# The last pair's second product: another order of the seven block products, one subtraction in two halves, one store issued from ScalarE

## The chip, the cores and the metric

The kernel runs on one core of one Trainium2 chip. The metric is the device time of one execution in microseconds (us), smaller is better. The kernel before has a median of 206.29 us over 6 runs (205.96 to 207.04).

## What is computed

Two stages follow each other. Attention with 4 batches, 8 heads, 768 tokens and head width 64: each token sees the 96 tokens up to itself and the first 8 tokens of its sequence, with a penalty that grows with distance. Then a feed-forward block on the 3072 tokens of width 512:

```
h = x @ w_in              # 3072 x 512  @  512 x 2048
g = h - np.tanh(h)
out = g @ w_out           # 3072 x 2048 @ 2048 x 512
```

The change touches the last line only, and of it the last 256 of the 3072 tokens.

## The kernel before, in words

The tokens are cut into 24 tiles of 128. The first four tiles go through the feed-forward block alone, the other twenty in ten pairs. A pair makes `g` (2048 x 256, bf16) in eight steps: TensorE (PE) multiplies by `w_in`, ScalarE (ACT) takes tanh, VectorE (DVE) subtracts.

The second product of a pair is done as two-by-two blocks with seven products in place of eight (function `by_strassen`). Let G(t,r) be tile t's part of `g` for half r of the 2048 rows, W(r,c) the block of `w_out` for row half r and column half c (256 of 512 columns). DVE first makes five sums of G blocks (operations ("A", g, kk), function `a_sum`, tile `hb`); the sums of W blocks (`bsum`) were made once, early. Then PE makes the products, 8 matmuls each into a PSUM bank:

- P4 = G(1,1)(W(1,0) - W(0,0)) and P3 = G(0,0)(W(0,1) - W(1,1)), in one bank, "in"
- P1 = (G(0,0) + G(1,1))(W(0,0) + W(1,1)), bank "one"
- P5 = (G(0,0) + G(0,1))W(1,1) and P2 = (G(1,0) + G(1,1))W(0,0), in one bank, "mid"
- P7 = (G(0,1) - G(1,1))(W(1,0) + W(1,1)); P6 = (G(1,0) - G(0,0))(W(0,0) + W(0,1)). In the last pair P7 has a bank of its own ("out2"), and P6 is made in two halves of 128 columns each, in two banks ("out" and "out3").

The blocks of the output are put together by a chain of operations, all but the first on DVE, each with a name in the code (key of the planner's operation):

- "s34" (ACT): copy P3 and P4 to `sum`. "t": tsum = P3 + P4. "u": tsum = P1 + tsum.
- "cx": the two cross blocks of the output, P5 + P3 and P2 + P4, 512 columns, into `ot2`.
- "ab": `sum` = tsum - cross, 512 columns: what is still missing in the two other blocks is only P7 and P6.
- "cs": the two other blocks, `ot2` = P7 or P6 + `sum`. In the last pair there are three: "out2" (256 columns, P7), "out" and "out3" (128 columns each, the halves of P6).
- Stores: in the last pair one of the two cross blocks after "cx" (256 KB, line 565), and one after each "cs" (128 KB, 64 KB, 64 KB, line 568). All are issued from SyncE's queue (SP). In the profile all DVE operations of this chain have line 324 and all matmuls of the products line 354, since helpers record them.

The order on each engine is not written by hand. A planner (class `Planner`) takes every operation with its engine, an assumed duration, what it comes after and which buffers it takes, and lays out a timetable; the instructions are then emitted engine by engine in that order. Order among the seven products is fixed by a list, ORDER = (4, 3, 1, 5, 2, 7, 6).

Of the kernel before, what the change touches and what calls it, by code (L numbers as in the profile page):

```python
# [13 lines left out]
PE, ACT, DVE, POOL, SP = ENG.PE, ENG.Activation, ENG.DVE, ENG.Pool, ENG.SP  # L14
# [158 lines left out]
def kernel(  # L173
# [11 lines left out]
    nc = tc.nc  # L185

    B, H, S, Dh = q.shape
    P = 128
# [41 lines left out]
    pl = Planner()  # L230
# [55 lines left out]
    DH = DM // 2  # L286
    LAST = len(groups) - 1
# [35 lines left out]
    def add(e, out, x, sign, y):  # L323
        eng_of(e).tensor_tensor(out=out, in0=x, in1=y, op=ALU.add if sign > 0 else ALU.subtract)  # L324
# [231 lines left out]
        assert r1 > r0  # L556
        nc.sync.dma_start(out=dst, in_=buf("ot2", ("ot2", g)))

    def store_part(g, part, c0=0, c1=DH):
        r0, r1 = [(tiles[u][0] * NQ + tiles[u][1]) * P for u in pair(g)]  # L560
        row = out.ap[0][0]
        src = buf("ot2", ("ot2", g))
        if part == "cross":
            dst = bass.AP(out.tensor, out.offset + r0 * row + DH, [[row, P], [(r1 - r0) * row - DH, 2], [1, DH]])
            nc.sync.dma_start(out=dst, in_=src.rearrange("q a d -> q (a d)")[:, DH : 3 * DH].rearrange("q (a d) -> q a d", a=2))
        else:
            r = (r0, r1)[part]
            nc.sync.dma_start(
                out=out[r : r + P, part * DH + c0 : part * DH + c1], in_=src[:, part, part * DH + c0 : part * DH + c1],
            )  # L570

# [19 lines left out]
    for g, us in enumerate(groups):  # L591
# [7 lines left out]
        out=ident, in0=rel, scalar1=0.0, scalar2=None, op0=ALU.is_equal), after=[("rel",)], pri=-3)  # L599
# [3 lines left out]
    for m in range(3):  # L603
        for half in range(2):
            pl.op(("mk", m, half), ACT, 0.85 if m or half else 2.15, lambda e, m=m, half=half: build_mask(m, half),
                  after=[("dist", m), ("mk", 0, 1) if m == 1 else None],
                  pri=-2 if m == 0 else 1)
# [4 lines left out]
    for it in arrive:  # L612
        nm, j = it[0], int(it[1:])
        if nm == "i":
            key = ("in", j)
            c0, w = in_from[j] * P, IN_PARTS[j]
            pl.op(key, POOL, 0.8, lambda e, j=j, c0=c0, w=w: nc.gpsimd.dma_start(  # L617
                out=w_in_bf[j], in_=w_in_r[:, :, c0 : c0 + w * P]),
                  after=[prev and ("issue", prev)], dma=T_W * w / 4 + (0.5 if j == 0 else 0.0) + (0.1 if w < 4 else 0.0), lag=W_LATE)
            prev = key  # L620
        elif nm == "o":
            key = ("out", j)
            pl.op(key, POOL, 0.8, lambda e, j=j: nc.gpsimd.dma_start(out=w_out_bf[j], in_=w_out_r[:, j * FJ : (j + 1) * FJ, :]),  # L623
                  after=[prev and ("issue", prev)], dma=T_W, lag=W_LATE)
            prev = key
        else:
            u = j
            src = {"k": k, "q": q, "v": v}[nm]
            key = ("ld", nm, u)
# [6 lines left out]
            if (nm, u) in hw_loads:  # L636
# [4 lines left out]
                          out=dst8(buf("kf", ("kf", nm, u)).rearrange("p h d -> p (h d)")) if u < N8 else buf("kf", ("kf", nm, u)),  # L641
# [4 lines left out]
                      lambda e, u=u, nm=nm, dst=dst: copy(e, dst(), buf("kf", ("kf", nm, u))),  # L646
# [12 lines left out]
    for u in range(NU):  # L659
# [64 lines left out]
        g = group_of[u]  # L724
# [16 lines left out]
                      out=buf(xname(g), ("xT", g))[:, :, off : off + P], in_=buf("x", ("x", u)).rearrange("q h d -> q (h d)")),  # L741
                  after=[("N", u, 0), ("N", u, 1), ("issue", prevx) if prevx else None], take=xt, give=[("x", u)], dma=T_TR, lag=LATE, pri=-1)

    ORDER = (4, 3, 1, 5, 2, 7, 6)
    for kk in (6, 4, 3, 1, 7):
        for j in range(2):
            pl.op(("B", kk, j), [(DVE, 0.602)], None, lambda e, kk=kk, j=j: b_sum(e, kk, j),
# [12 lines left out]
    def by_strassen(g):  # L760
        us = pair(g)
        per = shape1(g)[1] if g < PAIR0 else BANK // P
        p2 = 2 if g < PAIR0 else 1.5
        u0, u1 = us
        heads = [g] if g < PAIR0 else us
        gall = [("g", x, f) for x in heads for f in range(0, CF, per)]
        glow = [("g", x, f) for x in heads for f in range(0, CH, per)]
        for tag in gtags(g):
            pl.uses[tag] = 7
        for kk in (6, 1, 5, 2, 7):  # L770
            pl.op(("A", g, kk), [(DVE, 0.602)], None, lambda e, g=g, kk=kk: a_sum(e, g, kk),
                  after=glow if kk == 6 else gall, take=[("hb", ("a", g, kk))], give=gtags(g), pri=1)
        before_p = {4: gall, 3: [], 1: [("A", g, 1)], 5: [("A", g, 5)], 2: [("A", g, 2)],
                    7: [("A", g, 7)], 6: [("A", g, 6)]}
        last = None
        for kk in ORDER:
            bs = [("B", kk, j) for j in range(2)] if kk in B_OF else []
            n = home(g, kk)[0]
            opens = kk in (4, 1, 5, 7) or g == LAST and kk == 6
            halves = [0, 1] if g == LAST and kk == 6 else [1]  # L780
            for half in halves:
                two = len(halves) == 2
                key = ("P", g, kk) if half else ("Pp", g, kk)
                tag = "out3" if two and half else n
                c = (half * DH // 2, half * DH // 2 + DH // 2) if two else (0, DH)
                pl.op(key, PE, 0.45 if two else 0.875, lambda e, g=g, kk=kk, c=c, tag=tag: product(g, kk, c[0], c[1], tag),
                      after=before_p[kk] + bs + ([("issue", last)] if last else []),
                      take=[("bank", ("P", g, tag))] + ([("lim2", ("l2", g, n))] if g != LAST or kk in (4, 1, 5) else []) if opens else [],
                      give=(gtags(g) if kk in A_RAW else [("a", g, kk)]) if half else [], pri=p2, mode="full")
                last = key  # L790

        def bank(g, n):
            return buf("bank", ("P", g, n)).rearrange("q (a d) -> q a d", a=2)

        def one(g):
            return buf("bank", ("P", g, "one"))[:, 0:DH]

        def cross(g):
            return buf("ot2", ("ot2", g)).rearrange("q a d -> q (a d)")[:, DH : 3 * DH].rearrange("q (a d) -> q a d", a=2)

        def same(g):
            return bass_same(buf("ot2", ("ot2", g)))

        def sm(g):
            return buf("sum", ("s", g))

        def ts(g):
            return buf("tsum", ("t", g))

        pl.op(("s34", g), [(ACT, 0.483), (DVE, 0.6)], None, lambda e, g=g: copy(e, sm(g), bank(g, "in")),  # L810
              after=[("P", g, 3), ("P", g, 4)], take=[("sum", ("s", g))], give=[("P", g, "in"), ("l2", g, "in")], pri=1)
        pl.op(("t", g), DVE, 0.335, lambda e, g=g: add(e, ts(g), sm(g)[:, 0, :], 1, sm(g)[:, 1, :]),
              after=[("s34", g)], take=[("tsum", ("t", g))], pri=1)
        pl.op(("u", g), DVE, 0.335, lambda e, g=g: add(e, ts(g), one(g), 1, ts(g)),
              after=[("t", g), ("P", g, 1)], give=[("P", g, "one"), ("l2", g, "one")], pri=1)
        pl.op(("cx", g), DVE, 0.605, lambda e, g=g: add(e, cross(g), bank(g, "mid"), 1, sm(g)),
              after=[("P", g, 5), ("P", g, 2), ("s34", g)], take=[("ot2", ("ot2", g))],
              give=[("P", g, "mid"), ("l2", g, "mid")], pri=1)
        pl.op(("ab", g), DVE, 0.6, lambda e, g=g: add(
            e, sm(g), ts(g).rearrange("q (a d) -> q a d", a=1).to_broadcast([P, 2, DH]), -1, cross(g)),  # L820
              after=[("cx", g), ("u", g)], give=[("t", g)], pri=1)
        if g == LAST:
            pl.op(("st", u0), SP, 0.6, lambda e, g=g: store_part(g, "cross"), after=[("cx", g)], dma=T_ST)
            for t, c0, c1, key, tag in ((0, 0, DH, ("P", g, 7), "out2"), (1, 0, DH // 2, ("Pp", g, 6), "out"),
                                        (1, DH // 2, DH, ("P", g, 6), "out3")):
                end = tag == "out3"
                pl.op(("cs", g, tag), DVE, 0.335 if t == 0 else 0.2, lambda e, g=g, t=t, c0=c0, c1=c1, tag=tag: add(
                    e, buf("ot2", ("ot2", g))[:, t, t * DH + c0 : t * DH + c1], buf("bank", ("P", g, tag))[:, c0:c1], 1, sm(g)[:, t, c0:c1]),
                      after=[("ab", g), key], give=[("P", g, tag)] + ([("s", g)] if end else []), pri=1)
                pl.op(("st", us[t], tag), SP, 0.4, lambda e, g=g, t=t, c0=c0, c1=c1: store_part(g, t, c0, c1), after=[("cs", g, tag)],  # L830
                      give=[("ot2", g)] if end else [], dma=T_ST * (c1 - c0) / DM)
            return
        pl.op(("cs", g), DVE, 0.605, lambda e, g=g: add(e, same(g), bank(g, "out"), 1, sm(g)),
              after=[("ab", g), ("P", g, 7), ("P", g, 6)], give=[("P", g, "out"), ("l2", g, "out"), ("s", g)], pri=1)
        pl.op(("st", u0), SP, 0.6, lambda e, g=g: store2(g), after=[("cs", g)], give=[("ot2", g)], dma=2 * T_ST)
# [52 lines left out]
    seq2, share2 = [], []  # L888
    for g, us in enumerate(groups):
        if fast(g):  # L890
            seq2 += [("P", g, kk) for kk in ORDER]
            share2 += [us[0] + 2.0 * n / 7 for n in range(7)]
        elif g >= HEAD:
            for t in range(len(us)):
                n = 5 if us[t] == NU - 1 else 4
                seq2 += [("m2", g, t, qq) for qq in range(n)]
                share2 += [us[t] + qq / n for qq in range(n)]
# [61 lines left out]
```

## Time and profile before

| | us |
|---|---|
| median of 6 runs | 206.29 |
| the profiled execution's own time | 206.01 |
| its span, first to last instruction | 204.2 |
| PE busy over the span | 197.5 |
| DVE busy over the span | 183.8 |
| from 196.0 to 200.0: PE, DVE, ACT busy | 4.00, 3.24, 0.59 |
| from 200.0 to 204.2: PE, DVE, ACT busy | 0.35, 0.86, 0.00 |

The profile counts time from the span's start; the execution's own time is 1.8 us longer than its span. The columns of a timeline are start, duration, engine, line and operation, and out<-in by the program's names. A name with a q behind the engine (SPq) is the engine's queue that issues a DMA: the duration there is that of issuing, not of the transfer. Merged lines (x3) hold several instructions, from the first one's start to the last one's end. In the last stretch of the span, from 200.0 to 204.2, almost no engine computes.

### The profile page before, as it was taken

Reading aid. Unit: us, or ns where it says so; the run is one execution under the profiler, and the core shown is the slowest. Engines: PE = TensorE matmul, PEld = TensorE weight load, DVE = VectorE, ACT = ScalarE, POOL = GpSimd, SP = SyncE. Lnnn points to the kernel's source line nnn. Section 1 sums busy time; section 2 is a strip of 40 time slices with the busy share of each in tenths; the row PEclk is TensorE's granted clock in tenths of the full one; section 3 lists DMA queues with packets and bytes.
Section 4 is the critical chain, followed back from the end, with each engine's and each line's share of the span. In section 5 each row is a group of like instructions: output and inputs, shape, how many; then the busy total and the mean of one; then the engine's idle time right before and its main releaser. Section 6 shows DMA issues by size and latency. Waiting matters only on the chain.

```text
span 204.2 us, 6062 instructions
## 1 busy us (share of the span) xinstructions
PE 197.5 (97%) x2397; PEld 169.7 (83%) x2400; DVE 183.8 (90%) x408; ACT 138.8 (68%) x326; POOL 67.1 (33%) x83
## 2 busy tenths in 40 slices
PE   7999999999999999999999999999999999999992
PEld 5669989478798989888889888889888889888882
DVE  6799989999799899999898999898999899799683
ACT  5888889266796678559986548986648967534310
POOL 8993665360455310725040735040630000000000
PEclk9999999999999999999999999999999999999999
DMA  6999999999799995999998999996999222102023
GB/s 139 165 195 190 171 199 203 180 157 174 206 129 184 106 105 153 110 136 228 103 109 151 112 164 187 113 108 152 109 161 170 55 51 106 27 6 99 2 106 103
DMA packets 104429, 27.18 MB, mean 133 GB/s; under 512 B 94800, under 2 KB 101584, under 8 KB 104400
## 3 DMA queue, kind: packets, MB, share of 16 engines
q0 software_dynamic: 72416, 13.37, 86.5%
q1 hardware_dynamic: 31184, 13.11, 32.6%
q10 hardware_dynamic: 800, 0.30, 0.7%
q8 instruction: 19, 0.31, 0.6%
q14 instruction: 10, 0.08, 0.2%
HBM read 27.30 MB, written 6.29 MB: 164 GB/s over the span
## 4 chain that ended last, share of the span: by engine, by line
PE 79%; DMA 12%; POOL 5%; DVE 1%; issue 1%; DVEq 0%; POOLq 0%
PE bank L497 34%; PE bank L354 33%; DMA w_out_bf<-in_moe_w_out_dram 7%; DMA w_in_bf<-in_moe_w_in_dram 5%; PE bank L425 5%; PE bank L445 2%; PE bank L538 2%; PE bank L447 2%; POOL vb L654 2%; POOL w_in_bf L617 1%; POOL kb L652 1%; POOL qb L652 1%; DVE ot L324 1%; PE bank L482 0%; POOL w_out_bf L623 0%
## 5 line engine op out<-in xcount | busy, mean ns | idle before, releaser
L497 PE MATMUL bank<-xT,w_in_bf 128*128 128x256 bf16 (+1 forms) x896 | 93.3, 257 | 0.0
L497 PEld LDWEIGHTS <-w_in_bf 128*128 128x128 bf16 x896 | 76.1, 98 | 7.7
L850 ACT ACTIVATE th<-bank 128x512 f32<-128x512 f32 x96 | 57.3, 610 | 35.0 <-PE bank L497 33.2
L506 DVE TENSOR_TENSOR g<-bank,th 128x512 bf16<-128x512 f32 x80 | 53.4, 684 | 7.5 <-ACT th L850 6.4
L354 PEld LDWEIGHTS <-hb 128*128 128x128 bf16 x464 | 43.7, 98 | 5.6
L654 POOL DMA_DIRECT2D kb<-in_k_dram x20 | 17.7, 887 | 75.4 <-PE bank L497 59.0
L354 PE MATMUL bank<-bsum,hb 128*128 128x256 bf16 (+1 forms) x288 | 35.5, 270 | 0.0
L324 DVE TENSOR_TENSOR hb<-g 128x1024 bf16<-128x1024 bf16 x50 | 32.6, 686 | 0.4
L430 ACT ACTIVATE pd<-bank 128x512 bf16<-128x512 f32 x48 | 26.1, 599 | 7.5 <-PE bank L425 7.4
L354 PE MATMUL bank<-w_out_bf,hb 128*128 128x256 bf16 x176 | 22.7, 273 | 0.0
L654 POOL DMA_DIRECT2D vb<-in_v_dram x24 | 21.4, 895 | 2.3 <-DMA w_out_bf<-in_moe_w_out_dram 2.2
L430 ACT ACTIVATE po<-bank 128x512 bf16<-128x512 f32 x40 | 22.0, 614 | 0.0
L462 ACT ACTIVATE x<-bank,rden 128x64 bf16<-128x64 f32 x88 | 20.4, 326 | 2.0 <-DVE rden L454 1.7
L354 PE MATMUL bank<-bsum,g 128*128 128x256 bf16 x160 | 20.2, 273 | 0.0
L435 DVE TENSOR_TENSOR pd<-pd,mk 128x1024 bf16<-128x1024 bf16 (+1 forms) x30 | 17.0, 578 | 1.9 <-ACT pd L430 1.6
L654 POOL DMA_DIRECT2D qb<-in_q_dram x20 | 17.7, 888 | 0.9 <-PE bank L482 0.8
L354 PEld LDWEIGHTS <-g 128*128 128x128 bf16 x160 | 15.1, 98 | 2.4
L324 DVE TENSOR_TENSOR ot<-bank,sum 128x512 f32<-128x512 f32 (+2 forms) x24 | 15.2, 638 | 0.8 <-PE bank L354 0.6
L445 PE MATMUL bank<-vb,pd 128*128 128x65 bf16 x192 | 14.6, 193 | 0.6 <-DVE pd L435 0.5
L425 PE MATMUL bank<-qT,kT 64*128 64x128 bf16 x352 | 13.8, 217 | 0.6 <-DVE qT L415 0.6
L425 PEld LDWEIGHTS <-kT 64*128 64x128 bf16 x352 | 10.0, 94 | 4.9 <-issue 4.1
L435 DVE TENSOR_TENSOR po<-po,mk 128x1024 bf16<-128x1024 bf16 (+1 forms) x23 | 14.0, 616 | 0.0
(66 smaller groups left out, 178.2 us busy)
## 6 DMA issues: line engine op xcount, KB each, us to landing
out_dram<-ot SPq DMA_DIRECT2D x10, 512.0 KB, 4.4
vb<-in_v_dram POOLq DMA_DIRECT2D x24, 128.0 KB, 5.9
kb<-in_k_dram POOLq DMA_DIRECT2D x23, 128.0 KB, 4.7
qb<-in_q_dram POOLq DMA_DIRECT2D x23, 128.0 KB, 5.3
w_in_bf<-in_moe_w_in_dram POOLq DMA_DIRECT2D x4, 512.0 KB, 9.5
w_out_bf<-in_moe_w_out_dram POOLq DMA_DIRECT2D x4, 512.0 KB, 12.8
out_dram<-ot SPq DMA_DIRECT2D x3, 256.0 KB, 2.3
xT<-x SPq DMA_TRANSPOSE x18, 2.5
```

What stands on the lines that cost most here:

```text
L324: eng_of(e).tensor_tensor(out=out, in0=x, in1=y, op=ALU.add if sign > 0 else ALU.subtract)
L354: nc.tensor.matmul(o, a, b[:, c0:c1], start=(f == 0), stop=(f == CH - 1))
L425: nc.tensor.matmul(t[hh][:, p * P : (p + 1) * P], kt[r, p, :], qt[r, p, :], start=True, stop=True)
L430: nc.scalar.activation(dst, t, AF.Exp, bias=0.0, scale=scale)
L435: nc.vector.tensor_tensor(out=p, in0=p, in1=mk[:, m, s0 * NP : s1 * NP, :], op=ALU.mult)
L445: nc.tensor.matmul(o, pd[:, slot(h), :], vd[:, h, 0 : Dh + 1], start=True, stop=w is None)
L447: nc.tensor.matmul(o, buf("po", ("p", u, 1))[:, slot(h), :], bufs[vname(w)][got["vb", w]][:, h, 0 : Dh + 1], start=False, stop=True,)
L462: nc.scalar.activation(x[:, h, :], t[:, h, 0:Dh], AF.Copy, bias=0.0, scale=rd[:, h, :])
L497: nc.tensor.matmul(t[:, (f - fa) * n : (f - fa + 1) * n], w_in_bf[j][:, c, fo : fo + P], xt[:, c, 0:n], start=(c == 0), stop=(c == CD - 1),)
L506: nc.vector.tensor_tensor(out=dst, in0=t.rearrange("q (b n) -> q b n", n=n), in1=th.rearrange("q (b n) -> q b n", n=n), op=ALU.subtract,)
L654: else nc.gpsimd.dma_start(out=dst(), in_=rows(src, u)),
L850: pl.op(("th", g, f), ACT, 0.48, lambda e, g=g, f=f: nc.scalar.activation(buf("th", ("th", g, f)), buf("bank", ("h", g, f)), AF.Tanh, bias ...
```

## The change

Three edits, all in the last pair:

1. The order of its products becomes 4, 3, 5, 2, 1, 7, 6: P1 comes after P5 and P2 in place of before them. The order of the DVE sums that feed them follows (6, 5, 2, 1, 7). The other pairs keep theirs.
2. "ab" becomes two operations of 256 columns each, one per tile; each "cs" waits for its own half only.
3. The store of "out" (the first half of P6) is issued from ACT's queue; the two other stores of line 568 stay with SP.

Counts: DVE has one instruction more, SP one DMA less, ACT one DMA more; PE has the same instructions, 24 of them in another order. On DVE the order of the chain is t, cx, u, ab (twice), cs (three times); before it is t, u, cx, ab, cs (three times). All instructions ahead of this chain keep their order.

```diff
-    def store_part(g, part, c0=0, c1=DH):
+    def store_part(g, part, c0=0, c1=DH, e=SP):
...
-            nc.sync.dma_start(
+            (nc.scalar if e is ACT else nc.sync).dma_start(
                 out=out[r : r + P, part * DH + c0 : part * DH + c1], in_=src[:, part, part * DH + c0 : part * DH + c1],
             )
...
-    ORDER = (4, 3, 1, 5, 2, 7, 6)
+    def order_of(g):
+        return (4, 3, 5, 2, 1, 7, 6) if g == LAST else (4, 3, 1, 5, 2, 7, 6)
+
...
-        for kk in (6, 1, 5, 2, 7):
+        for kk in (6, 5, 2, 1, 7) if g == LAST else (6, 1, 5, 2, 7):
...
-        for kk in ORDER:
+        for kk in order_of(g):
...
-        pl.op(("ab", g), DVE, 0.6, lambda e, g=g: add(
-            e, sm(g), ts(g).rearrange("q (a d) -> q a d", a=1).to_broadcast([P, 2, DH]), -1, cross(g)),
-              after=[("cx", g), ("u", g)], give=[("t", g)], pri=1)
         if g == LAST:
+            pl.uses["t", g] = 2
+            for t in range(2):
+                pl.op(("ab", g, t), DVE, 0.335, lambda e, g=g, t=t: add(e, sm(g)[:, t, :], ts(g), -1, cross(g)[:, t, :]),
+                      after=[("cx", g), ("u", g)], give=[("t", g)], pri=t)
...
-                      after=[("ab", g), key], give=[("P", g, tag)] + ([("s", g)] if end else []), pri=1)
-                pl.op(("st", us[t], tag), SP, 0.4, lambda e, g=g, t=t, c0=c0, c1=c1: store_part(g, t, c0, c1), after=[("cs", g, tag)],
+                      after=[("ab", g, t), key], give=[("P", g, tag)] + ([("s", g)] if end else []), pri=0.5)
+                pl.op(("st", us[t], tag), ACT if tag == "out" else SP, 0.4, lambda e, g=g, t=t, c0=c0, c1=c1: store_part(g, t, c0, c1, e), after=[("cs", g, tag)],
                       give=[("ot2", g)] if end else [], dma=T_ST * (c1 - c0) / DM)
             return
+        pl.op(("ab", g), DVE, 0.6, lambda e, g=g: add(
+            e, sm(g), ts(g).rearrange("q (a d) -> q a d", a=1).to_broadcast([P, 2, DH]), -1, cross(g)),
+              after=[("cx", g), ("u", g)], give=[("t", g)], pri=1)
```

More of the change, by code (lines that the diff above doesn't have):

```diff
@@ L890 @@
         if fast(g):
-            seq2 += [("P", g, kk) for kk in ORDER]
+            seq2 += [("P", g, kk) for kk in order_of(g)]
             share2 += [us[0] + 2.0 * n / 7 for n in range(7)]
```

## The prediction

> **What bounds the kernel now.** First the page's busy shares and its chain that ended last: PE is busy nearly throughout and carries 79% of that chain, so the body of the kernel is PE's. The change leaves every instruction ahead of the last pair's closing chain in place, so only the end can pay or cost. I therefore read the end of the chain in order of time:
>
> ```profile
> PE 197.5 (97%) x2397; PEld 169.7 (83%) x2400; DVE 183.8 (90%) x408; ACT 138.8 (68%) x326; POOL 67.1 (33%) x83
> PE 79%; DMA 12%; POOL 5%; DVE 1%; issue 1%; DVEq 0%; POOLq 0%
> ...
> 192.47 6.13 PE bank L354 x56
> 198.62 0.70 DVE ot L324
> 199.34 0.70 DVE sum L324
> 200.09 0.04 issue
> 200.14 0.42 DVE ot L324
> ```
>
> PE makes 56 matmuls, seven products of 6.13/7 = 0.876 us each, without a gap. At 198.62, as soon as P2 has ended, the chain leaves PE for DVE: "cx", "ab", "cs". Three products are still to come, and yet PE is no longer what ends last. The timeline of the same stretch shows by how little, and what follows:
>
> ```profile
> 196.00 0.59 ACT L413 COPY sum<-bank 128x512 f32<-128x512 f32 x1 [2.90 <-PE bank L354]
> 196.67 1.91 PE L354 MATMUL bank<-w_out_bf,hb 128*128 128x256 bf16 x16
> 197.05 0.42 DVE L324 TENSOR_TENSOR tsum<-sum 128x256 f32<-128x256 f32 x1
> 197.58 0.42 DVE L324 TENSOR_TENSOR tsum<-bank,tsum 128x256 f32<-128x256 f32 x1
> 198.42 1.93 PE L354 MATMUL bank<-bsum,hb 128*128 128x256 bf16 x24
> 198.62 0.69 DVE L324 TENSOR_TENSOR ot<-bank,sum 128x512 f32<-128x512 f32 x1 [0.62 <-PE bank L354]
> 199.34 0.69 DVE L324 TENSOR_TENSOR sum<-tsum,ot 128x512 f32<-128x512 f32 x1
> 200.14 0.42 DVE L324 TENSOR_TENSOR ot<-bank,sum 128x256 f32<-128x256 f32 x1
> 200.48 0.48 DVE L324 TENSOR_TENSOR ot<-bank,sum 128x128 f32<-128x128 f32 x2
> ```
>
> SP's own lines of that time, and from the view of DMA issues the time from issue to landing (the cross store, "out2", the two 64 KB stores):
>
> ```profile
> 200.59 0.34 SPq L568 DMA_DIRECT2D out_dram<-ot  x1
> 201.03 0.38 SPq L568 DMA_DIRECT2D out_dram<-ot  x1
> 201.50 0.41 SPq L568 DMA_DIRECT2D out_dram<-ot  x1
> ...
> out_dram<-ot SPq DMA_DIRECT2D x1, 256.0 KB, 2.2
> out_dram<-ot SPq DMA_DIRECT2D x1, 128.0 KB, 1.7
> out_dram<-ot SPq DMA_DIRECT2D x2, 64.0 KB, 1.6
> ```
>
> Three things to see. PE ends at 198.42 + 1.93 = 200.35, but DVE ends at 200.96: the last sum ("out3") runs 0.6 us behind the product it reads. Then SP issues three stores 0.44 and 0.47 apart; the last is issued at 201.50, though its data was there at 200.96, so 0.54 us are spent queueing behind two other issues. It lands 1.6 us later, at about 203.1, and the closing takes the remaining 1.1 us to 204.2. The two 128-column sums at 200.48 have 0.48 us together; one alone lasts 281 ns, so their starts (200.48 and 200.68) are 0.20 apart, and the first starts 0.34 after the 256-column one, ahead of its end at 200.56.
>
> **The change part by part.**
>
> *Order 5, 2, 1.* PE has the same 24 matmuls, so its end stays at 200.35. P5 and P2 read sums that DVE makes first and second, as P1 and P5 do now; the sums end by 197.14, the places of the waits on PE are the same, and PE stood nowhere in this stretch, so this costs PE nothing. P2 ends one product sooner: "cx" is released at 198.62 - 0.876 = 197.75. DVE is free by then (its "t" runs 197.05 to 197.47, the copy on ACT ended at 196.59), so "cx" takes 0.69 to 198.44. "u" now waits for P1, which ends where P2 did: 198.62 to 199.04. Behind it on DVE queue only operations that need it. The cover for moving "u" late is the removed "cx"; late next is "ab".
>
> *"ab" in halves.* One 0.69 us operation goes, two of 0.42 us come (row: the 256-column "t" and "u"), but starts of successive operations are 0.34 apart where nothing is awaited. The first half waits for "u": the trace has 0.03 ("cx" to "ab", 199.31 to 199.34) and 0.11 ("ab" to "cs", 200.03 to 200.14) for such a step between dependent operations; I take 0.07: 199.11. The second half starts at 199.45, "out2" at 199.79 (P7 ended at about 199.45, its half of "ab" at 199.53), "out" at 200.13 (its half ended at 199.87), "out3" could at 200.33, but PE's last product ends at 200.35 and PE to DVE takes 0.04 (198.58 to 198.62): 200.39, ending 200.67. Against 200.96 that is 0.29 us less, and PE is then the bound again.
>
> The Trainium skill, "VectorE: DVE Perf Modes", section "The DRAIN you can't avoid", speaks against this edit: by it each operation starts only when the one before has drained, so more operations cost more (it adds that one which nothing holds starts earlier). The 128-column starts 0.20 apart for 0.28 long say otherwise here. By the rule the chain would run 199.11 + 3 x 0.42 + 2 x 0.28 = 200.93 at "out3", and the gain here would be 0.03, not 0.29.
>
> *The store of "out" from ACT.* ACT's last work ends at 196.59, so nothing is queued behind its wait. "out2" ends at 200.21 and SP issues at 200.24 (0.03, as 200.56 to 200.59), occupying SP until 200.68 by the 0.44 spacing. "out3" ends at 200.67, so its issue starts at 200.70 in place of 201.50: 0.80 us earlier. Of that, 0.29 is DVE's and 0.51 the queue's. ACT issues "out" at 200.44. ACT's own issues stand in the trace only at the start (0.71 us beside SP's 0.74 for the same shape), landing 3.3 us and 3.8 us after issue among other loads; SP's at the end take 0.34 to 0.41 and land after 1.6. The nearest row is SP's own store of the same 64 KB at the same idle time: 200.44 + 1.6 = 202.0, or 202.4 if the issue takes 0.71; both stay at or near "out3" at 200.70 + 1.6 = 202.3. The far end is a rival below.
>
> *Transfers closer together.* Now three stores pass in 201.43 to 202.75 with a pause of about 0.1 us before the last. From the issues they would begin at 201.08 ("out2"), 201.28 and 201.6. If all 256 KB run at the 345 GB/s of the cross store they need 0.75 us, ending 201.83, before "out3" would end alone (about 201.9): cost nothing. If they pass one behind another at the lengths they show now, some 0.40 + 0.45 + 0.35 us, the end is 202.28: 0.35 later. I take 0.10, near the low end, since "out3" begins only when "out2" is through. The cross store moves from 199.34 to 198.47 with "cx"; the 512 KB store ahead of it landed 2.7 us after 195.36, so it meets nothing.
>
> Sum: 0.29 + 0.51 - 0.10 = 0.70 us. From the profiled execution's 206.01 that gives 205.31; that run lies 0.28 below the median of 206.29, so the median goes to 205.59, say 205.6 (-0.34%). What a measurement of this kernel can tell from no change is about 0.3%, 0.62 us: the forecast lies just beyond it.
>
> **The rivals.**
>
> 1. DVE does not overlap the split operations. For: both halves write `sum` and read the same `tsum`, and the 0.11 step shows a stall between dependent operations. Against: 0.34 spacing between "out2" and "out". Then "out3" ends at 200.93 or so, its issue starts at 200.96, and 0.54 less 0.10 remains: 205.85.
> 2. The stores queue in the DMA engines: full 0.35, gain 0.45, 205.85; with a slower landing of 64 KB pieces mixed from two queues, another 0.2: 206.05.
> 3. The change does nothing: the store from ACT lands as late as the last one does now, 2.7 us after issue at 200.44. For: ACT's own rows are 3.3 and 3.8. Against: those ran among 128 KB to 256 KB loads at the start, where SP's landed even later, at 4.2. Result 206.3.
> 4. Slower: ACT's store lands as its rows at the start do. 200.44 + 3.3 to 3.8 = 203.74 to 204.24 against 203.1 now: 0.6 to 1.1 us more, 206.9 to 207.4. It decides from a landing of 2.7 us; the 0.71 us issue alone does not reach it.
>
> **How the numbers follow.** Chances: forecast 0.60, rival 1 0.13, rival 2 0.12, rival 3 0.06, rival 4 0.09. The forecast's own span is 205.45 to 205.75 by its bounds (gain 0.84 where DVE follows PE's modelled end at once and nothing queues, 0.54 where three quarters of the 0.35 are paid); medians of 6 scatter by some 0.15 more, as the runs cover 205.96 to 207.04. Faster by over 0.3%, below 205.67: 0.55 of the forecast's 0.60 and 0.08 of rivals 1 and 2 through scatter, 0.63. Slower: rival 4, 0.09. Within: the other 0.28. The range runs from 205.1 (the whole 0.84 and a median as far down as the profiled run was) to 206.3 (rival 3), leaving out rival 4 and a little on each side.
>
> **What the changed profile would show.** "cx" at 197.75, right behind the last sum of blocks and "t"; "u" at 198.62; two 256-column operations on `sum` 0.34 apart (0.42 or more would be rival 1); "out3" at 200.39 released by PE, the chain staying on PE to 200.35; two SP issues of line 568, the second at 200.7, and one ACT issue near 200.44; landings of 1.6 to 1.8 us (2.0 or more for "out3": rival 2; 2.7 or more for ACT's: rivals 3 and 4); span 203.5. The prediction is wrong if the span shrinks by 0.7 and the median does not follow, or if an earlier stretch moves although its instructions have the same order.

## The result and the profile after

The changed kernel has a median of 205.42 us (204.96 to 206.26, 21 runs) against 206.29 us before (205.51 to 207.34, 42 runs). The ratio is 0.9955, with a 95% interval of 0.9942 to 0.9967: 0.68 to 1.20 us of 206.29, all of it beyond the 0.62 us named in the prediction. (The ratios here are taken over all runs; the quotient of the two medians is 0.9958.) The profiled execution took 205.19 us (206.01 before), its span 203.4 us (204.2 before).

First the end of the chain that ended last, in order of time, of the kernel after (start, duration, engine and tile):

```profile
192.40 6.13 PE bank L354 x56
198.55 0.44 DVE tsum L324
199.01 0.48 DVE sum L324 x2
199.49 0.19 issue
199.69 0.14 DVE ot L324
199.83 0.19 issue
200.02 0.28 DVE ot L324
200.31 0.29 DVE ot L324
```

As before, PE carries the chain until a product ends and DVE takes over; it is now P1 that hands over, to "u", while "cx" is already behind it. In the two "issue" lines of 0.19 DVE is not idle: the second half of "ab" runs from 199.35 to 199.77, and "out2" from 199.69 to 200.11. The view follows DVE to the end and does not go back to PE for "out3". The timeline of the same stretch of the kernel after:

```profile
193.98 1.91 PE L354 MATMUL bank<-bsum,g 128*128 128x256 bf16 x16
195.73 1.91 PE L354 MATMUL bank<-w_out_bf,hb 128*128 128x256 bf16 x16
197.47 2.80 PE L354 MATMUL bank<-bsum,hb 128*128 128x256 bf16 x32
197.67 0.69 DVE L324 TENSOR_TENSOR ot<-bank,sum 128x512 f32<-128x512 f32 x1 [0.27 <-PE bank L354]
198.55 0.42 DVE L324 TENSOR_TENSOR tsum<-bank,tsum 128x256 f32<-128x256 f32 x1 [0.18 <-PE bank L354]
199.01 0.76 DVE L324 TENSOR_TENSOR sum<-tsum,ot 128x256 f32<-128x256 f32 x2
199.69 0.92 DVE L324 TENSOR_TENSOR ot<-bank,sum 128x256 f32<-128x256 f32 x3
200.31 0.29 DVE L324 TENSOR_TENSOR ot<-bank,sum 128x128 f32<-128x128 f32 x1
...
200.13 0.34 SPq L568 DMA_DIRECT2D out_dram<-ot  x1
200.33 0.36 ACTq L568 DMA_DIRECT2D out_dram<-ot  x1
200.63 0.34 SPq L568 DMA_DIRECT2D out_dram<-ot  x1
...
out_dram<-ot SPq DMA_DIRECT2D x1, 256.0 KB, 2.5
out_dram<-ot ACTq DMA_DIRECT2D x1, 64.0 KB, 1.8
out_dram<-ot SPq DMA_DIRECT2D x1, 64.0 KB, 1.7
```

The last three lines are from the view of DMA issues: the cross store, "out" and "out3", with the time from issue to landing. Read the timeline against the lines of before shown in the prediction. "cx" (197.67) comes before "u" (198.55); the two halves of "ab" span 0.76 us together, so they start 0.34 apart; PE ends at 197.47 + 2.80 = 200.27 and "out3" starts at 200.31. No view names what "out3" waited for, but the spacing tells: "out3" starts 0.29 after "out" (200.02), where before it started 0.20 after it, so something held it for about 0.1 us, and the end of the product that it reads lies 0.04 ahead of its start. I read this as PE bounding the sums again. "out3" ends at 200.60 and its store is issued at 200.63: it queues behind nothing. Before, it waited 0.54 us.

The body of a single execution ends a little earlier or later each time: P4 and P3 start at 193.98 here, at 194.05 before, and anywhere from 193.87 to 195.35 in the profiled executions below, all of which do the same work ahead of that point. So the ends are compared from that start on:

| us from the start of P4 and P3 | "out3" starts | last store issued | span ends | against before: issue, end |
|---|---|---|---|---|
| before | 6.63 | 7.45 | 10.15 | |
| after | 6.33 | 6.65 | 9.42 | -0.80, -0.73 |
| order alone | 6.36 | 7.18 | 9.96 | -0.27, -0.19 |
| store from ACT alone | 6.63 | 6.98 | 9.80 | -0.47, -0.35 |
| halves alone | 6.50 | 7.32 | 10.01 | -0.13, -0.14 |
| order and store from ACT | 6.37 | 6.72 | 9.58 | -0.73, -0.57 |
| order and halves | 6.34 | 7.06 | 9.78 | -0.39, -0.37 |
| after, "out3" from ACT | 6.34 | 6.66 | 9.53 | -0.79, -0.62 |
| after, P1 one place later | 7.11 | 7.46 | 10.33 | +0.01, +0.18 |
| after, without the store of "out" | 6.34 | 6.66 | 9.35 | -0.79, -0.80 |

The spans are given to 0.1 us, so the column of span ends, and with it the end in the last column, is good to about 0.1: a difference below that between issue and end, or between the ends of two rows, says nothing.

### The profile page after: what moved, and what is told of

Read it like the earlier page. It is cut to its first block, busy times and chain, and to the rows that moved or that the text cites. A ratio compares the mean times of both kernels' runs of the same rounds, so it can differ in the third digit from the quotient of the medians.

```text
span 203.4 us, 6064 instructions
## 1 busy us (share of the span) xinstructions
PE 197.3 (97%) x2397; PEld 169.7 (83%) x2400; DVE 183.5 (90%) x409; ACT 138.7 (68%) x326; POOL 67.1 (33%) x83
## 4 chain that ended last, share of the span: by engine, by line
PE 90%; DVE 4%; DMA 2%; POOL 1%; issue 1%; POOLq 0%
PE bank L497 42%; PE bank L354 33%; PE bank L425 6%; PE bank L538 3%; PE bank L445 3%; PE bank L447 2%; DMA qb<-in_q_dram 2%; PE bank L482 1%; DVE pd L435 1%; DVE kT L415 1%; PE bank L477 1%; DVE qT L415 1%; DVE x L464 1%; POOL kb L652 0%; DVE ot L324 0%
```

## The experiments

My theory was the prediction's: the end is set by DVE's chain, or by PE where DVE fits before it; then by SP's issues; then by the landing. Rival A: only the store from ACT pays. Rival B: DVE does not overlap split operations. Rival C: a store from ACT lands late. The first four experiments were timed beside the kernel before on one chip (206.35 us there), the last four on another (206.15 us). Each has one profile.

**Order alone.** The changed kernel with one subtraction and all stores from SP:

```diff
-            pl.uses["t", g] = 2
-            for t in range(2):
-                pl.op(("ab", g, t), DVE, 0.335, ...
+            pl.op(("ab", g), DVE, 0.6, ...
...
-                pl.op(("st", us[t], tag), ACT if tag == "out" else SP, 0.4, ...
+                pl.op(("st", us[t], tag), SP, 0.4, ...
```

> Only the order 4, 3, 5, 2, 1, 7, 6; one 512-column subtraction, all stores from SP. My theory (DVE chain, then SP's issues 0.44 to 0.47 apart, then landing): the cross sum starts one product (0.88 us) earlier, u after P1, out3 ends at about 200.69 on the time axis of the kernel before (200.96 there), the last store is issued at about 201.23 in place of 201.50: 0.27 us less than before. Rival A (only the store from ACT pays, the chain on DVE is covered): 0 less. Rival B (DVE does not overlap split operations, so one subtraction is the better form): 0.27 or more, at least as much as order and halves together.

Median 205.81 us against 206.35 on the same chip, ratio 0.997 (0.995 to 0.9991). The last issue comes 0.27 us earlier, as worked out. Rival A falls: the order alone is faster. Its timeline shows the step that the halves were to remove:

```profile
199.06 0.69 DVE L324 TENSOR_TENSOR sum<-tsum,ot 128x512 f32<-128x512 f32 x1
199.86 0.82 DVE L324 TENSOR_TENSOR ot<-bank,sum 128x256 f32<-128x256 f32 x3
200.31 1.32 SPq L568 DMA_DIRECT2D out_dram<-ot  x3
201.22 0.41 SPq L568 DMA_DIRECT2D out_dram<-ot  x1
```

From the end of "ab" (199.75) to "out2" 0.11 us pass, and the last of three issues starts 0.91 after the first, though "out3" ended at 200.68.

**The store from ACT alone.** Against the kernel before, with the change's `store_part`, which takes the queue as an argument:

```diff
...
-                pl.op(("st", us[t], tag), SP, 0.4, ... store_part(g, t, c0, c1), ...
+                pl.op(("st", us[t], tag), ACT if tag == "out" else SP, 0.4, ... store_part(g, t, c0, c1, e), ...
```

> Only the store of the first half of P6 is issued from ACT; order and subtraction as before. My theory: DVE as before (out3 ends at 200.96), SP has one issue less, the last issue starts at about 201.03 in place of 201.50: 0.47 us less, or 0.40 if the landing takes 0.1 longer. Rival A: this alone gives the whole 0.8 to 0.9 us. Rival C (ACT's first store after a long pause lands late): nothing less, or more time than before.

Median 205.83 us against 206.35, ratio 0.9966 (0.9945 to 0.9987). The last issue comes 0.47 us earlier; the store lands 1.8 us after it (1.6 before), and the end of the span gains 0.35. From the view of DMA issues of this kernel:

```profile
out_dram<-ot SPq DMA_DIRECT2D x1, 128.0 KB, 1.8
out_dram<-ot ACTq DMA_DIRECT2D x1, 64.0 KB, 1.8
out_dram<-ot SPq DMA_DIRECT2D x1, 64.0 KB, 1.8
```

The issue on ACT took 0.36 us (SP's 0.34 and 0.38), and its store landed after 1.8. Rival C falls, and rival A with it once more: this alone is not the whole.

**Halves alone.** Against the kernel before:

```diff
-        pl.op(("ab", g), DVE, 0.6, ...
+            pl.uses["t", g] = 2
+            for t in range(2):
+                pl.op(("ab", g, t), DVE, 0.335, ...
...
-                      after=[("ab", g), key], ...
+                      after=[("ab", g, t), key], ...
```

> Only the subtraction in two halves; order 4, 3, 1, 5, 2, 7, 6 and all stores from SP. My theory: starts 0.34 apart, so out2 starts at 200.02 in place of 200.14 and all that follows comes 0.12 us earlier: 0.12 us less than before. Rival B (each operation waits for the end of the one before): two times 0.42 in place of 0.69, 0.15 us more than before.

Median 206.24 us against 206.35, ratio 0.9981 (0.996 to 1.0002): the times do not tell it from no change. Its timeline does:

```profile
199.48 0.76 DVE L324 TENSOR_TENSOR sum<-tsum,ot 128x256 f32<-128x256 f32 x2
200.16 0.81 DVE L324 TENSOR_TENSOR ot<-bank,sum 128x256 f32<-128x256 f32 x3
201.51 0.40 SPq L568 DMA_DIRECT2D out_dram<-ot  x1
```

From the start of "ab" to the start of "out2" are 0.68 us (0.80 before): two steps of 0.34, with no stall between. Everything after comes 0.13 us earlier. Rival B falls.

**Order and the store from ACT.** The changed kernel without the halves:

```diff
-            pl.uses["t", g] = 2
-            for t in range(2):
-                pl.op(("ab", g, t), DVE, 0.335, ...
+            pl.op(("ab", g), DVE, 0.6, ...
...
```

> Order and the store from ACT, one subtraction of 512 columns. My theory: out3 ends at 200.69, out2 is issued from SP at 200.32, the last store at 200.76 in place of 201.50: 0.74 us less before any queueing in the transfers, 0.64 with 0.10 of it; the halves are worth the remaining 0.06. Rival B: as fast as the whole change or faster. Rival A: as the store from ACT alone.

Median 205.51 us against 206.35, ratio 0.9957 (0.9938 to 0.9975). The last issue comes 0.73 us earlier (0.74 expected) and the landing takes 1.8. Beside the whole change's 0.80, the halves are worth 0.07 of issue time here; their time is not told apart by the medians.

**Order and halves.** The changed kernel with all stores from SP:

```diff
-                pl.op(("st", us[t], tag), ACT if tag == "out" else SP, 0.4, ...
+                pl.op(("st", us[t], tag), SP, 0.4, ...
```

> The whole change but for the queue: all three stores of line 568 from SP. My theory: out3 ends as in the whole change, SP issues at 200.24, 200.68 and about 201.14 on the time axis of the kernel before, so 0.36 us less than before and about 0.45 more than the whole change. Rival A (the queue is everything): 0 less than before.

Median 205.87 us against 206.15, ratio 0.9978 (0.9961 to 0.9994). The last issue comes 0.39 us earlier where 0.36 was expected, and 0.41 after the whole change's. "out3" starts where it does in the whole change (6.34 and 6.33), so those 0.41 us are the queue's. Against the kernel before, "out3" starts only 0.29 sooner (6.34 against 6.63) and the last issue 0.39: with all stores on SP the last one waits for the two issues ahead of it, and the first of these, that of "out2", starts 0.39 sooner (200.47 - 194.32 = 6.15 against 6.54).

**"out3" from ACT, "out" from SP.** Against the changed kernel:

```diff
-                pl.op(("st", us[t], tag), ACT if tag == "out" else SP, 0.4, ...
+                pl.op(("st", us[t], tag), ACT if tag == "out3" else SP, 0.4, ...
```

> The whole change with the two 64 KB stores exchanged: out3, the last one, from ACT and out from SP. My theory: out3's issue starts at 200.70 either way and ACT's issue is as quick as SP's, so the time is that of the whole change within 0.1 us (0.7 to 0.9 us less than before). Rival C (a store from ACT lands later than one from SP): later by what ACT's landing has more; 1 us or more if it lands as ACT's loads at the start did (3.3 to 3.8 us after issue).

Median 205.51 us against 206.15, ratio 0.9972 (0.9949 to 0.9996). The last issue, now ACT's, starts at 6.66 against 6.65, lasts 0.36, and lands after 1.8 where SP's took 1.7 in the changed kernel. Here ACT's store is the one that the end waits for, so a late landing would have shown in full; it is about 0.1 us.

**P1 one place later.** Against the changed kernel:

```diff
-        return (4, 3, 5, 2, 1, 7, 6) if g == LAST else (4, 3, 1, 5, 2, 7, 6)
+        return (4, 3, 5, 2, 7, 1, 6) if g == LAST else (4, 3, 1, 5, 2, 7, 6)
...
-        for kk in (6, 5, 2, 1, 7) if g == LAST else (6, 1, 5, 2, 7):
+        for kk in (6, 5, 2, 7, 1) if g == LAST else (6, 1, 5, 2, 7):
```

> The whole change, but P1 one place later still: 4, 3, 5, 2, 7, 1, 6. PE has the same work. My theory (PE bounds the end only while DVE's chain fits before it): u starts 0.87 us later and the whole chain behind it moves, out3 ends at about 201.48 and the last store is issued at about 201.55: as slow as before or up to 0.15 us slower. If PE or the transfers bound the end whatever DVE does: as the whole change, 0.8 us less than before.

Median 206.45 us against 206.15, ratio 1.0004 (0.9981 to 1.0026). The gain is gone, with PE's work unchanged. The timeline:

```profile
200.31 0.42 DVE L324 TENSOR_TENSOR tsum<-bank,tsum 128x256 f32<-128x256 f32 x1 [1.05 <-PE bank L354]
200.77 0.76 DVE L324 TENSOR_TENSOR sum<-tsum,ot 128x256 f32<-128x256 f32 x2
201.44 0.81 DVE L324 TENSOR_TENSOR ot<-bank,sum 128x256 f32<-128x256 f32 x3
202.33 0.38 SPq L568 DMA_DIRECT2D out_dram<-ot  x1
```

DVE stands idle 1.05 us for P1, and then needs 1.67 us from "u" (200.31) to "out3" (started at 201.98, the last 0.28 us of the merged line), while PE has only P6 left. So of the three places of P1 that were run, one is good: late enough to let "cx" go first, early enough that 1.67 us of sums fit before PE ends. (P1 between P5 and P2 was not run.) In the changed kernel they start at 198.55 and PE ends 1.72 later: the fit is 0.05 us.

**Without the store of "out".** Against the changed kernel:

```diff
+                if tag == "out":
+                    continue
                 pl.op(("st", us[t], tag), ACT if tag == "out" else SP, 0.4, ...
```

> The whole change without the store of the first half of P6 (128 of 512 columns of 128 rows are not written). My theory: that store is off the path but for queueing among the transfers, so this is 0 to 0.15 us faster than the whole change and out3 lands 1.6 us after its issue in place of 1.7. If the store from ACT is what ends last: faster by more than that.

Median 205.64 us against 206.15, ratio 0.9979 (0.9958 to 1.0); the interval reaches 1.0, that is no change, the changed kernel was not timed beside it, and the two cannot be told apart by time. In the profile the last issue is at 6.66 as in the changed kernel, and its landing takes 1.6 us in place of 1.7 (1.59 and 1.69 in the trace's own nanoseconds). The queueing that the third store costs is thus about 0.1 us.

No complete version here beats the changed kernel: after PE's end only one sum, one issue, one landing and the closing are left, and of queueing among them only the 0.1 us of the third store.

## Why the prediction was right

It gave 205.6 us (-0.34%); measured are 205.42 (-0.42%), 0.03 below the forecast's own span (205.45 to 205.75), for which it allowed some 0.15 of scatter, and inside the range of 205.1 to 206.3. (The range's lower end, worked out, is 206.29 - 0.84 - 0.28 = 205.17; it was put a little lower.)

- *Order 5, 2, 1 costs PE nothing.* Right: 192.40 6.13 x56 after, 192.47 6.13 x56 before. "cx" starts 3.69 us after P4 and P3 (197.67 - 193.98); predicted were 197.75 - 194.05 = 3.70.
- *0.29 us on DVE.* Measured 0.30 ("out3" at 6.33 against 6.63). The step from "u" to the first half of "ab" took 0.04 where 0.07 was taken, and "out3" starts 0.04 after PE's end, as forecast. The order alone brings 0.27 of it. The halves alone bring 0.13, but with the order in place only about 0.03 at "out3", since PE is in the way; what they then bring at the last issue (0.07, or 0.12 with all stores on SP) comes mostly from the store of "out2", issued sooner on the same queue.
- *The chain on PE.* One sign failed: the forecast had the chain that ended last stay on PE to 200.35. The view leaves PE at 198.53, with P1, and goes on over "u", "ab" and the three "cs" on DVE. The two paths lie within 0.05 us of each other, and the view took DVE's. That "out3" waited for PE is read from its spacing and from P1's later place, not from the view.
- *0.51 us in the queue.* The last issue came 0.80 us earlier, of which 0.30 is DVE's: 0.50. The two experiments that differ only in the queue show 0.47 (order and halves as before) and 0.41 (both changed). So how the 0.80 divides depends on which edit is counted first: the two DVE edits bring 0.39 and the queue 0.41 on top, or the queue 0.47 and the DVE edits 0.33 on top.
- *0.10 us of queueing among transfers.* The landing of "out3" went from 1.6 to 1.7, and back to 1.6 without the store of "out". Rival 2's 0.35 did not come. Where the last issue follows that of "out2" by 0.44 us (the store from ACT alone; order and store from ACT; P1 one place later) in place of 0.50, the landing took 1.8. It also took 1.8 with "out3" from ACT, 0.51 after "out2" but only 0.07 after "out".
- *The cross store.* The forecast had it meet nothing. It landed 2.5 us after its issue where it took 2.2, and a 16 KB packet of the queue that the profile calls "instruction" ran in the same stretch (198.0 to 200.6); that the packet slowed it is not shown. It cost nothing: the three stores behind it landed later still.
- *ACT's issue.* 0.36 us and a landing of 1.8 us: near SP's row, which was the one taken, and far from the 0.71 and 3.3 to 3.8 us of ACT's own rows at the start. Rivals 3 and 4 rested on those rows; they held for loads issued in the first two microseconds, not here.
- *The drain rule* of the Trainium skill ("VectorE: DVE Perf Modes", section "The DRAIN you can't avoid") weighed against the halves. The halves start 0.34 apart for 0.42 long, so the row decided, and the experiment with the halves alone gained 0.13 where operations one behind another would have lost 0.15. What the section says of an operation that nothing holds is what these rows show.

The sum of 0.70 is the tail's: measured from P4 and P3 the span's end moved by 0.73. The medians moved by 0.87, and the interval (0.68 to 1.20) covers both. The rest, 0.14, lies within what the body of an execution scatters; I have no run that explains it otherwise.

## What to carry to other kernels

At a kernel's end, follow the last result back through each queue: an engine may be done 0.5 us before its store is even issued, because stores that matter less are issued first on the same queue. Order the last products by how long the chain behind each is, and give the last one the shortest; but find the place from which the chain no longer fits before the producer's end, since one place too far gave the whole gain back. Measure such a tail from a fixed point near it in single profiles, because the body's scatter (here 1.5 us in single executions with the same work ahead of it) is larger than the effect.

## What had not been expected

That one operation split in two makes a chain shorter, with no change of order, is not what a count of operations suggests, and the forecast for it (0.12; measured 0.13) rested on two rows alone. A 512-column subtraction followed by a sum that reads it costs its 0.69 us and 0.11 more before the next starts (199.75 to 199.86 with the order alone, 200.03 to 200.14 before). Two halves cost 0.34 each and no stall, 0.68 in place of 0.80: with the halves alone the first half, which "out2" reads, ends at 199.90, and "out2" starts at 200.16, behind the start of the second half by the same 0.34.
